# Two key masks on ScalarE, and weight sums and counts at other places, in a routed attention and experts kernel

## The chip, the cores and the metric

The kernel runs on one core of a Trainium2 chip. The metric is the device time of one execution in microseconds (us), as the median of several runs. One further execution was taken by the hardware profiler; its times of single instructions are the ones used here. TensorE (PE; PEld is its weight load) multiplies matrices, VectorE (DVE), ScalarE (ACT) and GpSimd (POOL) work elementwise, and SyncE (SP) issues most transfers. Each engine works through its own list of instructions in order and waits for others by semaphores.

## The reference

The reference is an attention whose queries and keys see each other only within one of 16 clusters, and behind it a layer of 8 experts in which each token goes to one of them:

```python
# q, k, v: (4, 8, 768, 64); centroids: (8, 16, 64)
q_assign = argmax(einsum('bhsd,hcd->bhsc', q_n, c_n)); k_assign likewise
scores = where(q_assign == k_assign, q @ k.T / 8, -1e9)
x = softmax(scores) @ v                      # -> x: (3072, 512)
expert = argmax(x @ w_gate)                  # 8 experts
y = relu(x[rows of e] @ w1[e]) @ w2[e]       # 512 -> 1024 -> 512
out = softmax(x @ w_gate)[expert] * y
```

## The kernel before

**Attention.** Two heads make a pair, and there are 16 pairs. A pair is worked in two halves of 384 queries (h) and six blocks of 128 keys (j). `score` (L438) gives one PSUM tile per (h, j): four float matmuls of keys and queries, then two bfloat16 matmuls of a key mask MK and a query mask MQ, which add nothing within a cluster and a large negative number outside it. ScalarE takes the exponential (L445), which frees the tile; there are three such tiles. `add_up` (L447) sums the exponentials on VectorE, and `attend` (L453) multiplies them by V after all twelve scores. The masks of the next pair are made meanwhile: `assign0` to `assign2` (L299 to L327) find each row's cluster on VectorE and leave it transposed as ohT, and `place` (L329) writes MK and MQ on ScalarE.

The first pair has no such cover. `start_first` (L345) works it in two halves of rows: `clusters(h)` (L388) does the assignment of one half and then `place_half` (L373) writes the masks of that half, spread over the engines. An index g names a strip: 0 and 1 are query strips, 2 and 3 key strips, and a is the head. Key masks of even g are written by VectorE, of odd g by GpSimd (L383); of the query masks of the first half, strip 0 is written by ScalarE and strip 1 by GpSimd (L380), those of the second half by GpSimd.

**Experts.** The tokens are handled in ten groups, s = 0 to 9, each of one expert and of a fixed size: `EARLY` = 288, 288 and `RANKED` = 256, 288, 288, 384, 416, 416, 448, 128 rows. Groups 0 and 1 use tokens of the first three batches only, so that they can start while the last batch's routing is still being computed inside group 0. All groups but the last compute the first layer (`layer1`, L948) by a form of Strassen's scheme: twice (j = 0, 1) seven products of quarter matrices on TensorE (L969). It needs sums of quarters of the weights, `w1_sums` (L809), A[2], A[1], A[0], A[3] in this order, and of the transposed rows, `turn_rows` (L776, xT) and `x_sums` (L791, xc). From group 1 on, each pair of row tiles of the second layer (`layer2`, L1052, products at L1070) does the same with `w2_sums` (L913, V[0] to V[3]; V[1] needs V[0], V[3] needs V[1]) and `h_sums` (L1026). Rows beyond that pair go through `tile_of` (L1081, matmuls at L1089): 32 or 64 rows within the pair's work, a whole tile of 128 behind it. All sums are made by VectorE through `strassen` (L788).

In both layers a product goes on adding to a PSUM bank that another engine has to read first. In `layer2` the products come in the order a, d, b, a, c, d, c. The addition `add(z1[:, H:], c, p7)` (L927 in the profile) reads bank c between its two products, and the second c product waits for it. `layer1` has the same place with `add(block(1, 1), ...)`.

**The order of other work.** It is written out by hand. After each product `hook()` runs a list of functions: h1 is the first layer's list of lists (14 places, 0 to 6 for j = 0, 7 to 13 for j = 1), h2 the second layer's. Place 1 of a pair in `layer2` lies behind the d product, 2 behind b, 3 behind a, 4 behind the first addition to z1, 5 behind the second, 6 behind the last c product. The functions of a place are issued in the order in which `at(list, place, function, ...)` (L1172) entered them. For the sums of the next group the tuple `when` (L1214 to L1218) gives six places, for A[2], A[1], A[0], A[3], V[2], V[0]. Groups with s >= 2 take the third tuple if the next group has 256 rows or more, so 2 to 7 do. `turn_rows` stands at place 3 of h2 and `x_sums` at 4 (for group 1 both at 1).

Within group 0, `choose` (L564) ends with the tile `last`, `count` (L588) multiplies it on TensorE (L592, L593), and `number` (L595) turns the counts into places, from which GpSimd writes the tokens' entries (L607). Beside them stand `weigh` (L755, xw) and the sums of group 1. Group 0's second layer has no pairs; its places come after every second of eight steps of a whole tile.

Of the kernel before, what the change touches and what calls it, by code (L numbers as in the profile page):

```python
# [12 lines left out]
AF = mybir.ActivationFunctionType  # L13
# [20 lines left out]
def kernel(  # L34
# [11 lines left out]
    nc = tc.nc  # L46
    B, H, S, D = q.shape
# [120 lines left out]
    with tc.manual_schedule(), ExitStack() as actx:  # L168
# [103 lines left out]
        QT, KT, SIM, OH = {}, {}, {}, {}  # L272
# [8 lines left out]
        ksc2 = consts.tile([P, 2], F32)  # L281
        kscn2 = consts.tile([P, 2], F32)
# [16 lines left out]
        def assign0(n, part=1):  # L299

            sim = asg.tile([P, HI, 2 * C], F32, name="sim")[:, 0 : HI // part]
            nc.vector.transpose(sim.rearrange("p i c -> p (i c)"), SIM.pop(n)[:, 0 : HS // part])
            SIM[n] = sim.rearrange("p i (a c) -> p (i a) c", c=C)
# [41 lines left out]
        def start_first():  # L345
            HQ = HS // 2
            cps = ps_m.tile([P, 512], F32, name="mps")
            ps = [ps_s.tile([P, 2, 512], F32, name="sps") for _ in range(2)]
            src = [d.pop(0) for d in (QIN, KIN)]
            dst = [qkt.tile([P, S], F32, name=name) for name in ("qT", "kT")]  # L350
            QT[0], KT[0] = dst

            def turned(w, h):
                for j in range(NQ // 2):
                    for a in range(2):
                        nc.tensor.matmul(  # L356
                            ps[w][D * a : D * (a + 1), h, P * j : P * (j + 1)], lhsT=src[w][:, a, NQ // 2 * h + j, :], rhs=ident,
                            start=True, stop=True,
                        )

            def copied(w, h):
                nc.scalar.copy(dst[w][:, HS * h : HS * (h + 1)], ps[w][:, h, 0:HS])

            def similar_half(h):
                sps = SIM[0] = ps_m.tile([P, 512], F32, name="mps")
                for g in range(4):
                    c0 = HS * h + HQ * (g % 2)
                    nc.tensor.matmul(
                        sps[Q4 * g : Q4 * (g + 1), 0:HQ], lhsT=cT[:, 0].rearrange("p a c -> p (a c)"),
                        rhs=dst[g // 2][:, c0 : c0 + HQ], start=True, stop=True,  # L370
                    )

            def place_half(h, w):  # L373
                for g in (2 * w, 2 * w + 1):
                    for a in range(2):
                        c0 = HS * h + HQ * (g % 2)
                        to = (MQ, MK)[w][0][D * a : D * a + Q4, c0 : c0 + HQ]
                        rows = slice(Q4 * g, Q4 * (g + 1))
                        if w == 0:
                            (nc.gpsimd.tensor_copy if h or g else nc.scalar.copy)(to, OH[0][rows])  # L380
                        else:

                            (nc.gpsimd if g % 2 else nc.vector).tensor_scalar(  # L383
                                to, OH[0][rows], scalar1=ksc2[rows, a : a + 1], scalar2=kscn2[rows, a : a + 1],
                                op0=ALU.mult, op1=ALU.add,
                            )

            def clusters(h):  # L388
                assign0(0, 2)
                assign1(0, 2)  # L390
                assign2(0, 2)
                for w in (h, 1 - h):
                    place_half(h, w)

            turned(0, 0)
            copied(0, 0)
            turned(1, 0)
            copied(1, 0)
            warm = consts.tile([P, 1], F32)
            nc.scalar.activation(warm, cnrm, AF.Exp, scale=0.0)  # L400
            nc.tensor.transpose(cps[:, 0:P], cn.rearrange("p a d -> p (a d)"), ident)
            cv = cps[:, 0:P].rearrange("p (h a c) -> p h a c", a=2, c=C)
            for a in range(2):
                nc.vector.tensor_copy(cT[D * a : D * (a + 1), :, a, :], cv[D * a : D * (a + 1), :, a, :])
            turned(0, 1)
            copied(0, 1)
            similar_half(0)
            turned(1, 1)
            copied(1, 1)
            clusters(0)  # L410
            score_half(0, 0, 0, True)
            similar_half(1)
            for j in (1, 2):
                score_half(0, 0, j, True)
            clusters(1)
            OH.pop(0)
            for a in range(2):
                nc.sync.dma_start(
                    out=cn_d.rearrange("(h a) d c -> a d h c", a=2)[a], in_=cT[D * a : D * (a + 1), :, a, :]
                )  # L420
# [474 lines left out]
    with tc.manual_schedule(), ExitStack() as ectx:  # L895
# [265 lines left out]
        def first_weights(s):  # L1161
            if s >= len(EARLY):
                expert(s)
            GR[s]["w1"] = fetch1(GR[s]["e"], (wa, wb)[s % 2])

        def second_weights(s):
            GR[s]["w2"] = fetch2(GR[s]["e"], (wa, wb)[s % 2])

        for s in range(NS):
            h1, h2 = {}, {}  # L1170

            def at(d, i, f, *a):  # L1172
                d.setdefault(i, []).append(lambda: f(*a))

            if s == 0:
                at(h1, 3, sum_up, n - 1)
                at(h1, 3, weights_of, n - 1)
                at(h1, 4, gate, B - 1)
                at(h1, 4, gate_exp, B - 1)
                at(h1, 5, gate_sum, B - 1)  # L1180
                at(h1, 5, choose, B - 1)
                at(h1, 8, count, B - 1)
                at(h1, 9, number, B - 1)
                at(h1, 11, rows, n - 1)
                at(h1, 11, store, n - 1)
                at(h1, 12, rank_all)
                at(h2, 0, rank_rest)
                at(h2, 3, places, 2)
                at(h2, 3, first_weights, 2)
                at(h2, 5, places, 3)  # L1190
                at(h2, 7, indices, 2)
                at(h2, 7, gather, 2)
            if s == 3:
                at(h1, 12, ask)
                at(h2, 4, answer)
            if s < last:
                if s == 0:
                    first_weights(1)
                elif s > 1:
                    take(s + 1)  # L1200
                if s == 1:
                    at(h1, 6, weigh, 2)
                    at(h1, 7, take, 2)
                    at(h1, 8, second_weights, 2)
                else:
                    second_weights(s + 1)
                if 0 < s <= last - 2:
                    at(h2, 0, first_weights, s + 2)

                if 0 < s <= last - 3:  # L1210
                    at(h2, 1, places, s + 3)

                if s == 0:
                    when = ((h2, 1), (h2, 2), (h2, 5), (h2, 6), (h2, 7), (h2, 7))  # L1214
                elif s == 1:
                    when = ((h1, 9), (h1, 12), (h2, 2), (h2, 3), (h2, 6), (h2, 6))
                else:
                    when = ((h1, 9), (h1, 10), (h2, 1), (h2, 2), (h2, 2), (h2, 5))  # L1218
                if GR[s + 1]["T"] >= 2 * P:
                    for (h, i), f, a in zip(when, (w1_sums,) * 4 + (w2_sums,) * 2, (2, 1, 0, 3, 2, 0)):  # L1220
                        at(h, i, f, s + 1, (a,), nc.vector)
                at(h2, 1 if s == 1 else 3, turn_rows, s + 1)
                if GR[s + 1]["T"] >= 2 * P:
                    at(h2, 1 if s == 1 else 4, x_sums, s + 1)
            if s == 0:
                at(h1, 2, gather, 1)
                at(h1, 8, weigh, 1, slice(0, 1))
                at(h1, 11, weigh, 1, slice(1, 2))
                at(h1, 12, weigh, 1, slice(2, 3))
                at(h1, 12, take, 1)  # L1230
            elif s + 2 <= last:
                at(h1, 5 if s == 2 else 4, indices, s + 2)
                at(h1, 5 if s == 2 else 4, gather, s + 2)
                at(h2, 6 if s == 1 else 4, weigh, s + 2)
            if pairs_of(s):
                at(h1, 4, w2_sums, s, (1,), nc.vector)

                at(h1, 5 if s == 1 else 6, w2_sums, s, (3,), nc.vector)
            if s == last - 1:

                at(h1, 4, nc.gpsimd.drain)
            (layer1 if GR[s]["T"] >= 2 * P else few_columns)(s, h1)
            h_sums(s)
            layer2(s, h2)
# [271 lines left out]
```

## Time and profile before

| | |
|---|---|
| median of 3 runs | 657.68 us (657.41 to 657.73) |
| the profiled execution | 657.44 us, its span 655.7 us |
| mean granted TensorE clock | 0.999 |
| attention, first pair to first expert product | 0 to 328.4 us |
| expert group 0 | 328.4 to 360.15 us |
| groups 1 to 9 | 360.15 us to the end |
| W1 or W2 sum on VectorE (L789, 128x1024) | 1.20 to 1.23 us |
| exponential on ScalarE (L445, 128x768) | 0.81 us |
| key mask, 32x192: VectorE / GpSimd (L383) | 346 / 504 ns (median) |
| key mask, 32x384: ScalarE (L340) | 700 ns |
| query mask, 32x192 / 32x384: ScalarE (L380, L337) | 350 / 510 ns |

A line of a timeline reads: start in us from the span's start, duration in us, engine, line, operation, output <- inputs, shapes, count (xN merges N in a row, and the duration runs from the first start to the last end), and in brackets the idle time of the engine in front of it and what ended it. Matmuls are pipelined, so neighbouring rows of PE overlap; the distance from start to start is the step. A float matmul counts as two.

### The profile page before, as it was taken

Reading aid. Unit: us, or ns where it says so; the run is one execution under the profiler, and the core shown is the slowest. Engines: PE = TensorE matmul, PEld = TensorE weight load, DVE = VectorE, ACT = ScalarE, POOL = GpSimd, SP = SyncE. Lnnn points to the kernel's source line nnn. Section 1 sums busy time; section 2 is a strip of 40 time slices with the busy share of each in tenths; the row PEclk is TensorE's granted clock in tenths of the full one; section 3 lists DMA queues with packets and bytes.
Section 4 is the critical chain, followed back from the end, with each engine's and each line's share of the span. In section 5 each row is a group of like instructions: output and inputs, shape, how many; then the busy total and the mean of one; then the engine's idle time right before and its main releaser. Section 6 shows DMA issues by size and latency. Waiting matters only on the chain.

```text
span 655.7 us, 11490 instructions
## 1 busy us (share of the span) xinstructions
PE 643.5 (98%) x4252; PEld 423.0 (65%) x4252; DVE 489.5 (75%) x845; ACT 338.3 (52%) x584; POOL 133.0 (20%) x166
## 2 busy tenths in 40 slices
PE   8999999999999999999999999999999999999995
PEld 4454544445444454444494989989897977869773
DVE  6988878998889988999977987888869365572300
ACT  5677877768778677867532433334241331413210
POOL 5500000022000300033013612324241422140010
PEclk9999999999999999999999999999999999999999
DMA  7753445443455433329476498667694836614010
GB/s 150 162 104 73 79 92 98 74 80 62 79 98 98 74 74 72 74 33 334 110 274 195 152 335 283 232 254 234 241 309 157 281 131 184 229 66 168 8 49 19
DMA packets 189760, 95.38 MB, mean 145 GB/s; under 512 B 152895, under 2 KB 171839, under 8 KB 188416
## 3 DMA queue, kind: packets, MB, share of 16 engines
q1 hardware_dynamic: 184624, 81.56, 45.4%
q0 software_dynamic: 4928, 12.97, 6.0%
q8 instruction: 35, 0.57, 0.4%
q14 instruction: 29, 0.24, 0.1%
q10 hardware_dynamic: 144, 0.03, 0.0%
HBM read 74.10 MB, written 20.70 MB: 145 GB/s over the span
## 4 chain that ended last, share of the span: by engine, by line
PE 94%; DVE 4%; issue 0%; ACT 0%; POOL 0%; POOLq 0%; DVEq 0%; ACTq 0%
PE sps L433 24%; PE mps L457 19%; PE bank L969 12%; PE bank L1089 10%; PE sbank L969 9%; PE bank L1070 7%; PE sbank L1070 6%; PE mps L480 3%; PE mps L291 2%; PE bank L938 1%; DVE xT L780 1%; DVE a L789 1%; DVE v L789 1%; PE sps L356 0%; PE sps L226 0%
## 5 line engine op out<-in xcount | busy, mean ns | idle before, releaser
L445 ACT ACTIVATE A<-sps 128x768 f32<-128x768 f32 x192 | 151.7, 814 | 29.1 <-PE sps L433 28.5
L433 PE MATMUL sps<-qT,kT 64*128 64x384 f32 x768 | 158.9, 492 | 0.0
L451 DVE TENSOR_TENSOR acc<-acc,A 128x768 f32<-128x768 f32 x128 | 121.3, 948 | 10.6 <-ACT A L445 2.4
L457 PE MATMUL mps<-A,v_in 128*64 128x384 f32 x768 | 127.4, 488 | 0.0
L433 PEld LDWEIGHTS sps<-qT,kT 64*128 64x128 f32 x768 | 66.8, 187 | 52.2 <-issue 46.0
L457 PEld LDWEIGHTS mps<-A,v_in 128*64 128x64 f32 x768 | 53.8, 137 | 70.6 <-issue 64.2
L1044 POOL DMA_INDIRECT out_dram<-z,si x30 | 47.1, 1571 | 195.3 <-DVE z L927 165.7
L607 POOL DMA_INDIRECT tokens_of<-tg,pos_i x24 | 28.2, 1176 | 268.5 <-DVE pos_i L605 262.4
L433 PE MATMUL sps<-mq,mk 64*128 64x384 bf16 x384 | 64.6, 323 | 1.6 <-DVE mk L383 1.0
L1089 PE MATMUL bank<-w,h 128*128 128x512 f32 (+2 forms) x224 | 64.4, 596 | 0.0
L340 ACT ACTIVATE mk<-ohT,kscn,ksc 32x384 bf16<-32x384 bf16 x60 | 42.0, 700 | 40.2 <-DVE ohT L327 36.3
L738 POOL DMA_INDIRECT xg<-x_rows,gi x30 | 40.3, 1343 | 45.8 <-DVE si L729 16.5
L969 PE MATMUL sbank<-xc,a 128*128 128x144 f32 (+4 forms) x288 | 47.9, 309 | 0.2 <-ACT sbank L1002 0.2
L969 PE MATMUL bank<-xT,w 128*128 128x144 f32 (+4 forms) x288 | 47.6, 308 | 0.0
L1089 PEld LDWEIGHTS bank<-w,h 128*128 128x128 f32 (+2 forms) x224 | 24.6, 151 | 32.5 <-issue 32.3
L969 PEld LDWEIGHTS bank<-xT,w 128*128 128x128 f32 x288 | 43.8, 190 | 2.3 <-issue 1.9
L451 DVE TENSOR_TENSOR acc<-A 128x768 f32<-128x768 f32 x32 | 30.6, 957 | 18.3 <-ACT A L445 18.2
L969 PEld LDWEIGHTS sbank<-xc,a 128*128 128x128 f32 x288 | 43.3, 190 | 0.7 <-ACT sbank L1002 0.4
L927 DVE TENSOR_TENSOR h<-sbank,p 128x288 f32<-128x288 f32 (+4 forms) x18 | 9.2, 513 | 45.3 <-PE sbank L969 43.9
L987 ACT ACTIVATE h<-h 128x288 f32<-128x288 f32 (+4 forms) x36 | 17.6, 488 | 40.2 <-DVE h L927 38.1
L433 PEld LDWEIGHTS <-mk 64*128 64x128 bf16 x384 | 19.9, 94 | 27.5 <-DVE mk L383 2.6
L755 DVE TENSOR_TENSOR xw<-xg,sf 128x256 f32<-128x256 f32 (+2 forms) x60 | 32.6, 603 | 0.2
(216 smaller groups left out, 898.7 us busy)
## 6 DMA issues: line engine op xcount, KB each, us to landing
w<-in_moe_w_dram SPq DMA_DIRECT2D x20, 2048.0 KB
v_in<-in_v_dram SPq DMA_DIRECT2D x32, 192.0 KB
x_rows<-x SPq DMA_DIRECT2D x64, 96.0 KB
turn_rows<-xw SPq DMA_DIRECT2D x23, 256.0 KB
q_in<-in_q_dram SPq DMA_DIRECT2D x60, 96.0 KB
k_in<-in_k_dram SPq DMA_DIRECT2D x60, 96.0 KB
xs<-turn_rows SPq DMA_DIRECT2D x16, 144.0 KB
xs<-turn_rows SPq DMA_DIRECT2D x8, 208.0 KB
```

The costliest lines, as they stand in the source:

```text
L340: nc.scalar.activation(dst, src, AF.Identity, bias=less, scale=big)
L433: nc.tensor.matmul(SP[n, h, j][:, a, 0:HS], lhsT=kt[rows, j * P : (j + 1) * P], rhs=qt[rows, h * HS : (h + 1) * HS], start=first, stop=not ...
L445: nc.scalar.activation(A[n, h, j], ps[:, :, 0:HS], AF.Exp, scale=D**-0.5)
L451: nc.vector.tensor_tensor(ACC[n, h], first, A[n, h, j], op=ALU.add)
L457: nc.tensor.matmul(O[n, h][D * a : D * (a + 1), 0:HS], lhsT=VIN[n][:, a, j, :], rhs=A[n, h, j][:, a, :], start=(j == 0), stop=(j == NQ - 1),)
L607: ins = nc.gpsimd.indirect_dma_start(out=t_d[:, :], out_offset=bass.IndirectOffsetOnAxis(ap=pos_i[:, i : i + 1], axis=0), in_=tg[:, b, i, ...
L738: nc.gpsimd.indirect_dma_start(out=xg[0:m], out_offset=None, in_=x_d[0:rows_in, :], in_offset=bass.IndirectOffsetOnAxis(ap=g["gi"][0:m, j ...
L755: nc.vector.tensor_tensor(xw[0:m, :, :, d2 * a : d2 * (a + 1)], xg[0:m].rearrange("p (r a d b) -> p a r b d", r=HP, a=2, b=DB)[:, a], g["s ...
L969: nc.tensor.matmul(ps[:, f * T2 : (f + 1) * T2], lhsT=w[:, k, (2 * j + f) * P : (2 * j + f + 1) * P], rhs=x[:, k, :], start=first and f + ...
L1044: ins = nc.gpsimd.indirect_dma_start(out=out[:, :], out_offset=bass.IndirectOffsetOnAxis(ap=GR[s]["si"][0:rows, j : j + 1], axis=0), in_=z ...
L1070: nc.tensor.matmul(ps[:, 0:H], lhsT=x[:, k, :], rhs=y[:, k, :], start=first and k == 0, stop=k == 3, skip_group_check=not first,)
L1089: nc.tensor.matmul(ps[i * m : (i + 1) * m, :], lhsT=h[:, f, j * P : j * P + m], rhs=w[:, f, :], start=(k == 0), stop=(k == FB // n - 1),)
```

## The change

Three places. In `place_half` the two key masks of strip 2 of the first half (h = 0) are written by ScalarE, as an Identity activation with the same scale and bias. In group 0, `count` and `number` stand one place later. And two of the `when` tuples change: for group 0 A[1] moves from place 2 to 1, A[0] from 5 to 2, A[3] from 6 to 2 and V[2] from 7 to 6; for groups 2 to 7 V[2] moves from 2 to 5 and V[0] from 5 to 6.

```diff
                         if w == 0:
                             (nc.gpsimd.tensor_copy if h or g else nc.scalar.copy)(to, OH[0][rows])
+                        elif h + g == 2:
+
+                            nc.scalar.activation(
+                                to, OH[0][rows], AF.Identity, bias=kscn2[rows, a : a + 1], scale=ksc2[rows, a : a + 1]
+                            )
                         else:
-
                             (nc.gpsimd if g % 2 else nc.vector).tensor_scalar(
...
-                at(h1, 8, count, B - 1)
-                at(h1, 9, number, B - 1)
+                at(h1, 9, count, B - 1)
+                at(h1, 10, number, B - 1)
...
                 if s == 0:
-                    when = ((h2, 1), (h2, 2), (h2, 5), (h2, 6), (h2, 7), (h2, 7))
+                    when = ((h2, 1), (h2, 1), (h2, 2), (h2, 2), (h2, 6), (h2, 7))
                 elif s == 1:
                     when = ((h1, 9), (h1, 12), (h2, 2), (h2, 3), (h2, 6), (h2, 6))
                 else:
-                    when = ((h1, 9), (h1, 10), (h2, 1), (h2, 2), (h2, 2), (h2, 5))
+                    when = ((h1, 9), (h1, 10), (h2, 1), (h2, 2), (h2, 5), (h2, 6))
```

## The prediction

> **What bounds the kernel now.** I read the page's busy shares first, then the chain of work that ended last, then the waits of TensorE, and then the timeline around each wait.
>
> ```profile
> PE 643.5 (98%) x4252; PEld 423.0 (65%) x4252; DVE 489.5 (75%) x845; ACT 338.3 (52%) x584; POOL 133.0 (20%) x166
> ...
> PE 94%; DVE 4%; issue 0%; ACT 0%; POOL 0%; POOLq 0%; DVEq 0%; ACTq 0%
> ```
>
> TensorE is busy for 643.5 of 655.7 us and carries 94% of the chain. The granted clock is 0.999. No edit here removes a matmul, so only the roughly 12 us in which TensorE stands still can be won. The waits of TensorE (us in total, times, longest) say where:
>
> ```profile
> PE sbank L1070 <- DVE z L927: 1.2, 4, 0.4
> PE sps L433 <- DVE mk L383: 1.0, 1, 1.0
> PE mps L592 <- DVE last L586: 0.6, 1, 0.6
> PE sbank L969 <- DVE h L927: 0.5, 1, 0.5
> ```
>
> All four end on VectorE, and each edit lies beside one of them. A wait is worth more than its number, because the overlap of neighbouring matmul groups is lost too. So I measure each from starts to starts in the timeline, against the same step where it runs unhindered.
>
> **Start: two key masks go to ScalarE.** The timeline of before:
>
> ```profile
> 10.81 0.72 ACT L380 COPY mq<-ohT 32x192 bf16<-32x192 bf16 x2 [1.50 <-DVE ohT L327]
> 10.88 0.82 DVE L383 TENSOR_SCALAR mk<-ohT,ksc,kscn 32x192 bf16<-32x192 bf16 x2
> ...
> 12.13 0.81 ACT L445 ACTIVATE A<-sps 128x768 f32<-128x768 f32 x1 [0.60 <-PE sps L433]
> ...
> 14.67 0.68 DVE L383 TENSOR_SCALAR mk<-ohT,ksc,kscn 32x192 bf16<-32x192 bf16 x2
> ...
> 15.04 0.70 PE L433 MATMUL sps<-mq,mk 64*128 64x384 bf16 x2 [1.00 <-DVE mk L383]
> ```
>
> VectorE loses the two masks of 10.88, and its next work, the second half's assignment (11.73 on), waits for nothing else: it moves up by 11.73 - 10.88 = 0.85 us. The second half's masks are then ready for TensorE at 14.2 instead of 15.04.
>
> ScalarE gains two masks behind its two query copies, in front of the first exponential. This shape has no row there. The copies give the slope: 510 ns at 384 columns, 350 at 192, so 160 for 192 columns. The mask of 384 columns (L340) takes 700, so 192 take an estimated 540 ns. Bounds: 350 (the copy, no multiply) and 700. The masks run from 11.55 to 12.65. In before the second one ended at 11.70 and the exponential began 0.43 later, so it now begins at about 13.08 and ends at 13.89. Its end frees the PSUM tile for the fourth score matmul (13.07 before, 0.13 after the first exponential's end): 14.02. The mask matmul follows 0.65 to 0.75 later: 14.7 instead of 15.04. ScalarE agrees: two more exponentials (1.51) end at 15.42, against the 15.77 at which the fourth began. Gain 0.35 us; with 350 ns per mask 0.7, with 700 none. GpSimd's mask work (11.74 to 12.84) is not moved and still ends in front of the third score's need.
>
> Here a rule speaks against the change: the Trainium skill, page "ScalarE: Activation LUTs", section "Rules for kernel authors", sends multiplies and adds to VectorE, up to about three times as fast per element in bf16. The row has a median of 346 ns on VectorE, so by three times a mask would cost 1040 on ScalarE, the exponential would start 1.0 us later than I have it, and the start would lose 0.65. I take the slope of the rows, which gives a factor of 1.6.
>
> One more wait follows. In the second pair the step from the first score group to the sums takes 31.00 to 33.96, in the third pair 51.08 to 53.70: 0.34 more, because ScalarE's query masks come late behind "DVE ohT" (its 28.14 row waits for that). VectorE has no idle gap between 11.73 and 28.02, so that transpose comes 0.85 us earlier while TensorE comes 0.35 earlier. The 0.34 goes. Start in all: 0.7 us (0 to 1.1). The loads don't hold it: the first 14 us moved 2.4 MB, all that these transposes read.
>
> **First expert group: count and number one product later.**
>
> ```profile
> 339.10 0.17 DVE L586 CAST last<-pr 128x8 bf16<-128x8 f32 x1
> 339.19 1.13 DVE L755 TENSOR_TENSOR xw<-xg,sf 128x256 f32<-128x256 f32 x2
> 339.33 0.17 PE L592 MATMUL mps<-last,lt_b 128*128 128x8 bf16 x1 [0.59 <-DVE last L586]
> ```
>
> The product that starts at 337.59 ends its step at 338.57 (0.98 each), then TensorE waits for "last". The next product could run: it needs nothing of VectorE. Moved in front, it ends its step at 339.55, after "last" (339.27). From 337.59 to the product at 340.44 are 2.85 us; two products and about 0.1 for the count matmuls are 2.06. Gain 0.79. The step "number" reads the count on VectorE at 340.22, behind the xw pair there; its place in VectorE's order doesn't change (the built order shows it), and the count is ready at about 339.85. So its six indirect writes, and the SyncE loads behind them, are not later. The cover is 0.28 us; without it some of the wait returns.
>
> **First group, second layer: weight sums earlier.** Two W1 sums move in front of the transpose xT, where VectorE waits 3.67 us for the DMA of xs (355.81): 2.4 us of work, hidden. Behind the x sums then stand only two W2 sums.
>
> ```profile
> 363.93 2.35 DVE L789 TENSOR_TENSOR v<-w 128x1024 f32<-128x1024 f32 x2
> ...
> 366.20 0.45 DVE L927 TENSOR_TENSOR h<-sbank,p 128x288 f32<-128x288 f32 x1
> ...
> 366.71 1.25 PE L969 MATMUL sbank<-xT,a 128*128 128x144 f32 x8 [0.52 <-DVE h L927]
> ```
>
> Without the 2.4 us the addition of 366.20 comes when its product ends, at 365.2, and TensorE doesn't wait. 365.05 to 367.79 is 2.74, unhindered 1.96: gain 0.78. Both w2 and w1 of this group have landed by 342 (DMA idle then), so the earlier sums don't wait for them. The index steps for group 2's gather now have one sum (1.2) in front of them rather than two W1 sums, so GpSimd's gather and what SyncE issues behind it come no later.
>
> **Groups 2 to 7: one W2 sum leaves the place in front of xT.**
>
> ```profile
> 466.27 1.21 DVE L789 TENSOR_TENSOR v<-w 128x1024 f32<-128x1024 f32 x1
> 467.19 1.89 PE L1070 MATMUL bank<-v,h 128*128 128x256 f32 x8
> 467.40 1.76 DVE L780 STREAM_TRANSPOSE xT<-xs 128x1536 f32<-128x1536 f32 x1
> 469.10 0.37 DVE L927 TENSOR_TENSOR z<-sbank,p 128x256 f32<-128x256 f32 x1
> 469.52 1.99 PE L1070 MATMUL sbank<-w,hs 128*128 128x256 f32 x8 [0.44 <-DVE z L927]
> ```
>
> The last product writes the bank that "z" reads, so it waits for VectorE's queue. The step from the product before it to the product after it, less two free steps of 1.73: group 2, 3.85 - 3.46 = 0.39; group 4, 4.17 - 3.46 = 0.71; group 6, 0.48; group 7, 0.61; groups 3 and 5 nothing (0 to 0.1). Taking a sum (1.13 from start to start) out is more than any of these: in group 4 "z" starts at 467.97 and must end by 468.92. In group 2 the sum also waits 1.95 us for its weights, which no longer stands in front. Gain 2.19. What is late next: both W2 sums (2.3 us) now stand behind "z<-bank,u", and the next group's first addition behind them. VectorE's total in front of that addition is the same as before, but TensorE arrives earlier. Group 4 has 0.76 us of idle there and TensorE comes 0.71 earlier; group 2 keeps about 0.3; group 3 has 0.32 and TensorE comes no earlier; groups 5 to 7 have a whole output tile (6.87) between. No cost, but it is tight. Of the queues, SyncE alone changes its order: one load of a word of xe falls behind three writes of turned rows, which are issued earlier; nothing there is near TensorE.
>
> **Sum.** 0.69 + 0.79 + 0.78 + 2.19 = 4.45 us. The profiled execution took 657.44 (span 655.7), so 653.0; the median of the runs is 657.68, so 653.2. What a measurement can tell from no change is 0.2%, 1.3 us.
>
> **Rivals.**
> *The start gives nothing.* ScalarE's masks cost 700 ns or more and the first exponential eats what VectorE wins. For it: the first exponential then stands behind four operations instead of two. Against: the slope. Time: 657.68 - 3.76 = 653.9; by the rule's 1040 ns 654.2 (1.0 of the 4.45 lost).
> *The experts' stalls come back.* The tight places of groups 2 to 4 each take back what the group won, or the count waits again: about half of 3.76 is lost, 655.1. For it: the covers of 0.05 to 0.3 us. Against: behind the addition there are some 0.5 us more until TensorE needs it.
> *Slower.* The pair of W2 sums becomes a block in front of the next group's addition in groups 2, 3 and 4, which have no output tile in between. To lose it must cost 2.4 us per sum rather than 1.2 (contention with GpSimd's writes that start there): 3 x (2.4 - 0.5) = 5.7 lost against 4.45 won, 658.9. It decides once the block ends some 2 us later than I have it. Against: the 1.20 to 1.23 of every such row.
> *It does not do what it says*: the built order shows each move, so I give this no time of its own.
>
> **How the numbers follow.** All parts as computed 0.56; start without gain 0.16; stalls half back 0.16; within 0.2% 0.06; slower 0.06. Faster by over 0.2% is 0.88. The range goes from 652.2 (start at its best, and the 0.2 wait of L1002 gone too) to 655.8.
>
> **What would show it.** TensorE's waits on L383, L592, "h" L927, and all but one of those on "z" L927 (group 1 stays) gone; the mask matmul of 15.04 at about 14.7; the first exponential near 13.1; the mask row on ScalarE near 540 ns. Wrong if "sbank L969 <- DVE h" grows in groups 3 to 5, or the fourth exponential is not earlier than 15.77.

## The result and the profile after

The changed kernel takes 651.76 us (median of 6 runs, 651.37 to 652.41) against 657.69 us (657.08 to 658.26) of before in the same runs: a ratio of 0.9912 (95% interval 0.99 to 0.9924), so 5.9 us less (5.0 to 6.6). The forecast was 653.2 with a range from 652.2 to 655.8. The gain was there, and larger: 5.9 us where 4.45 were foretold, and the time lies just below the range.

The page's busy line of after, and the waits of TensorE (us in total, times, longest):

```profile
PE 641.4 (99%) x4252; PEld 422.9 (65%) x4252; DVE 488.6 (75%) x843; ACT 339.7 (52%) x586; POOL 139.1 (21%) x166
```

```profile
PE sps L226 <- DVE mq L219: 1.4, 1, 1.4
PE sps L437 <- ACT mk L383: 0.8, 2, 0.6
PE sps L437 <- ACT A L449: 0.3, 1, 0.3
PE sbank L1074 <- DVE z L931: 0.2, 1, 0.2
```

(Lines behind the edit stand 4 later than in before.) TensorE is busy for 641.4 us in a span of 650.6. All four waits that the prediction read out are gone: on VectorE's mask (1.0), on "last" (0.6), on "h" (0.5), and of those on "z" only group 1's 0.2 is left. Gone too are 0.5 on GpSimd's masks and 0.2 on L1002. New are 0.8 and 0.3 on ScalarE, in the first pair. The timeline of after there:

```profile
10.94 0.38 DVE L327 STREAM_TRANSPOSE ohT<-oh 128x192 bf16<-128x192 bf16 x1
...
12.09 1.10 ACT L383 ACTIVATE mk<-ohT,kscn,ksc 32x192 bf16<-32x192 bf16 x2
...
13.62 2.92 ACT L449 ACTIVATE A<-sps 128x768 f32<-128x768 f32 x4 [0.43 <-PE sps L437]
...
14.48 0.92 PE L437 MATMUL sps<-qT,kT 64*128 64x384 f32 x4 [0.25 <-ACT A L449]
15.23 0.33 PE L437 MATMUL sps<-mq,mk 64*128 64x384 bf16 x2
15.39 0.81 PE L437 MATMUL sps<-qT,kT 64*128 64x384 f32 x4
```

This execution began 0.54 us late: ohT is at 10.94, in before at 10.40 (the first transposes on TensorE took longer; in the other profiles ohT lies between 9.69 and 10.99). In the frame of before the first exponential starts at 13.62 - 0.54 = 13.08 and the mask matmul at 14.69. And group 4's second layer, where before had a W2 sum at 466.27 in front of xT:

```profile
462.77 1.76 DVE L784 STREAM_TRANSPOSE xT<-xs 128x1536 f32<-128x1536 f32 x1
464.05 1.89 PE L1074 MATMUL bank<-v,h 128*128 128x256 f32 x8
464.46 0.37 DVE L931 TENSOR_TENSOR z<-sbank,p 128x256 f32<-128x256 f32 x1
...
465.77 1.89 PE L1074 MATMUL sbank<-w,hs 128*128 128x256 f32 x8
```

"z" is done at 464.83, 0.94 us ahead of the product that needs it, and that product starts one free step (1.72) behind the one before.

The starts of TensorE's products, after against before, give this sum (us):

| step | foretold | measured in the traces |
|---|---|---|
| first pair, from ohT to the first sums | 0.35 | 0.61 |
| second pair | 0.34 | 0.34 |
| count and number | 0.79 | 0.76 |
| sums in group 0 | 0.78 | 0.78 |
| groups 2, 4, 6, 7 | 0.39, 0.71, 0.48, 0.61 | 0.40, 0.70, 0.49, 0.62 |
| group 3, first layer | none | 0.48 |
| pair 14 to pair 15 | none | 0.31 |
| sum | 4.45 | 5.49 |

Less the late beginning (0.54) that is 4.95; TensorE's last block of products starts at 637.12 instead of 642.08, 4.96 earlier.

### The profile page after: what moved, and what is told of

Same layout as the page of the kernel before. It is cut to its first block, busy times and chain, and to the rows that moved or that the text cites. A ratio compares the mean times of both kernels' runs of the same rounds, so it can differ in the third digit from the quotient of the medians.

```text
span 650.6 us, 11481 instructions
## 1 busy us (share of the span) xinstructions
PE 641.4 (99%) x4252; PEld 422.9 (65%) x4252; DVE 488.6 (75%) x843; ACT 339.7 (52%) x586; POOL 139.1 (21%) x166
## 4 chain that ended last, share of the span: by engine, by line
PE 98%; DVE 1%; ACT 0%; issue 0%; POOL 0%; POOLq 0%; DVEq 0%
PE sps L437 25%; PE mps L461 19%; PE bank L973 13%; PE bank L1093 10%; PE sbank L973 10%; PE bank L1074 8%; PE sbank L1074 6%; PE mps L484 3%; PE mps L291 2%; PE bank L942 1%; PE sps L356 1%; PE sps L226 0%; DVE a L793 0%; ACT mk L383 0%; ACT A L449 0%; PE sbank L907 0%
## 5 line engine op out<-in xcount | busy, mean ns | idle before, releaser
L1048 POOL DMA_INDIRECT out_dram<-z,si x30 | 52.0, 1732 | 188.1 <-DVE z L931 161.2
L742 POOL DMA_INDIRECT xg<-x_rows,gi x30 | 40.2, 1342 | 42.5 <-DVE si L733 14.3
```

The costliest lines, as they stand in the source:

```text
L742: nc.gpsimd.indirect_dma_start(out=xg[0:m], out_offset=None, in_=x_d[0:rows_in, :], in_offset=bass.IndirectOffsetOnAxis(ap=g["gi"][0:m, j ...
L1048: ins = nc.gpsimd.indirect_dma_start(out=out[:, :], out_offset=bass.IndirectOffsetOnAxis(ap=GR[s]["si"][0:rows, j : j + 1], axis=0), in_=z ...
```

## The experiments

Fifteen runs on four chips. In the expectations letters name theories; each expectation says what its letter means. Times are medians, gains are worked out from the ratio to before on the same chip and its interval, and need not equal the difference of the medians. The question of the first four: which part holds the excess?

**e1_masks**: before with the diff of `place_half` alone.

> Only the two key masks on ScalarE. Theory A (the four parts add up; what the prediction missed lies in small waits it did not count): the start is worth 0.95 us, the 0.69 foreseen and 0.26 that was missed because the second mask of the second half made TensorE wait once more (15.04 to 15.40), so 656.7. Theory B (the rest of the gain is an accident of the two profiled executions and the runs around them): 0.69, so 657.0. Theory C (the missed 1.5 us sit in the start, which the profile of the changed kernel hides by a later start): 655.5 or less. In the profile: the step from the second pair's first scores to its sums 2.62 instead of 2.96 under all of them.

656.47 us against 658.28: 2.1 us faster (1.4 to 2.8). More than the 0.95 that the first two pairs of the traces of before and after show, or the 1.26 with pair 15.

**e2_count**:

```diff
-                at(h1, 8, count, B - 1)
-                at(h1, 9, number, B - 1)
+                at(h1, 9, count, B - 1)
+                at(h1, 10, number, B - 1)
```

> Only count and number one place later. A and B: 0.79 us less, 656.9; the wait of L592 gone, nothing later in the trace changed. If the missed gain sat here (an earlier start of something that depends on the counts): 656 or less.

657.32: 0.9 us faster (0.3 to 1.6), in the trace 0.76.

**e3_group0**:

```diff
-                    when = ((h2, 1), (h2, 2), (h2, 5), (h2, 6), (h2, 7), (h2, 7))
+                    when = ((h2, 1), (h2, 1), (h2, 2), (h2, 2), (h2, 6), (h2, 7))
```

> Only the sums' places in group 0. A and B: 0.78 us less, 656.9; the wait of the product of 366.71 gone, the other waits as before.

657.44: 0.7 us faster (1.5 to none). As expected, though the interval does not exclude nothing.

**e4_groups27**:

```diff
-                    when = ((h1, 9), (h1, 10), (h2, 1), (h2, 2), (h2, 2), (h2, 5))
+                    when = ((h1, 9), (h1, 10), (h2, 1), (h2, 2), (h2, 5), (h2, 6))
```

> Only the places of the two W2 sums in groups 2 to 7. A and B: 2.19 us less, 655.5, in groups 2, 4, 6 and 7 with 0.39, 0.71, 0.48 and 0.61. If the 0.48 of group 3's first layer (the wait of L1002 at 425.38 in before) belongs to this edit, 655.0 and that wait is gone here and still there in the other three.

655.58: 3.2 us faster (2.1 to 4.3). In its trace the groups give 0.40, 0.48 (group 3), 0.70, 0.49 and 0.62, so 2.7. Group 3's step is thus part of this edit.

The profile of e4, which has VectorE's masks, showed something that the profile of before had not: from 15.3 to 18.7 us TensorE had half its clock. From this came theory D: TensorE's standstill there lets the clock fall in some executions.

**c_nomasks**: the changed kernel without the diff of `place_half`.

> The changed kernel with the two key masks back on VectorE: everything but the start's edit. Theory A (each part is worth what the traces' starts show, 0.95 us for the masks: 0.61 in the first pair, 0.34 in the second, and 0.3 more near pair 15): 0.95 to 1.25 us slower than the changed kernel, so about 5.0 us faster than before. Theory D (without the mask edit TensorE stands still around 11 to 15 us, and in some executions the granted clock then falls to 0.50 for 3.3 us, which costs 1.6 us when it happens): 1.3 to 2.5 us slower than the changed kernel in the median, with a wider spread, and mean clocks down to 0.994 in some of its runs where the changed kernel never falls under 0.997. In the profile: the wait of TensorE for the mask of VectorE at 15 us is back (1.0 us), the first step of the second pair is 2.96 again, and the step from pair 14 to 15 is 20.27 again rather than 19.95.

**p_after**: the changed kernel again, on the chip of c_nomasks.

> The changed kernel again, on the chip of the other three. Theory A: 5.2 us faster than before (start 0.95, pair 15 0.3, count 0.76, group 0 0.78, groups 2 to 7 2.2 without the wait of group 3, and up to 0.5 for that one). Theory D: up to 6.9 us, the sum of the four single edits on their chip, where before shows its wider spread. In the profile no clock under 1.0 in the first 26 us, and the end of the query copies of GpSimd at 2.3 us again rather than 1.5.

c_nomasks takes 653.61 us (652.93 to 654.02), p_after 651.49 (651.01 to 652.35), before 657.6. So the masks are worth 2.1 us here too, and the two ranges do not touch; this is what theory D expected (1.3 to 2.5) and more than A did. p_after is 6.2 us faster than before (5.0 to 7.4), which does not tell the two apart. In the profile of c_nomasks VectorE's mask holds TensorE for 1.0 us again and the step from pair 14 to 15 is 20.27, as expected; but the step of the second pair stays at 2.62, where 2.96 was expected (see p_before). The stretches of c_nomasks (busy of each engine, then the granted clock in the third column from the end, DMA share, GB/s):

```profile
14.00:15.00 1.00, 0.27 (x1) 0.09 (x1) 0.93 (x3) 0.47 (x1) 0.55 (x1) 1.00 0.35 45
15.00:16.00 1.00, 0.97 (x6) 0.69 (x7) 0.97 (x3) 0.54 (x1) 0.84 (x2) 0.68 0.16 12
16.00:17.00 1.00, 1.00 (x7) 0.69 (x4) 1.00 (x3) 0.27 (x1) 0.90 (x3) 0.50 0.19 25
17.00:18.00 1.00, 1.00 (x5) 0.47 (x4) 0.90 (x2) 0.81 (x1) 0.95 (x1) 0.50 0.00 0
18.00:19.00 1.00, 1.00 (x8) 0.86 (x6) 0.90 (x2) 0.40 (x1) 0.86 (x4) 0.61 0.00 0
```

TensorE stands still for 0.73 us of the stretch from 14 to 15, the last part of a gap of 1.00, and 0.6 us behind it the clock falls to 0.50, from 15.36 to 18.77. That is 3.41 us, not the 3.3 that the expectations have, and it is 3.41 in all five profiles that show a fall at the start. In p_after it is busy for 0.75 there, and the clock stays:

```profile
14.00:15.00 1.00, 0.75 (x5) 0.40 (x6) 0.90 (x4) 1.00 (x3) 0.80 (x2) 1.00 0.33 40
15.00:16.00 1.00, 1.00 (x10) 0.50 (x8) 1.00 (x2) 1.00 (x3) 0.90 (x3) 1.00 0.12 17
```

From ohT to the first sums are 14.40 us in c_nomasks, 13.2 in seven profiles with VectorE's masks and no fall of the clock, 12.71 in the one profile of before that the prediction had, and 12.0 to 12.1 with ScalarE's masks written once.

**f_fill**: before, with idle matmuls in the gap.

```diff
+            if n + h == 0 and j == 3:
+                for _ in range(14):
+                    nc.tensor.matmul(SP[-1][:, 0, HS:512], lhsT=MK[1][:, 0:P], rhs=MQ[1][:, 0:P], start=True, stop=True)
             score_half(n, h, j, False)
...
```

(`SP[-1]` is the tile of the score before.)

> Before, with 14 small bfloat16 matmuls (128 columns, zeros, into columns that nothing reads) put on TensorE in front of the first score that waits for VectorE's mask of the second half, where it stands still from 14.0 to 15.0 us. They take an estimated 0.8 us of that gap and release nothing. Theory A (only the waits count): same as before, within 0.3 us. Theory D (the standstill lets the clock fall in some executions): the clock never falls at 15 us in any run, no mean clock under 0.997, and the median is 0.5 to 1.5 us faster than before.

656.39: 1.2 us faster (0.7 to 1.7), but not as meant. The matmuls waited 0.79 us for the exponential that reads that tile, the clock fell in the profile at 14.3 all the same, and they put the masked score 1.3 us later. In its profile three waits of the experts (0.8, 0.4 and 0.5 us in groups 0, 2 and 3) were absent, which nothing in the edit explains; such waits come and go from one execution to the next, as is shown below. As a test of D it failed. Still, of its 22 runs the profiled one alone has a mean clock of 0.996 or less.

**g_fill2**: 8 matmuls, into a tile that ScalarE doesn't read.

```diff
...
+            if n + h == 0 and j == 3:
+                for _ in range(8):
+                    nc.tensor.matmul(SIM[-1][:, HS:512], lhsT=MK[1][:, 0:P], rhs=MQ[1][:, 0:P], start=True, stop=True)
```

(`SIM[-1]` is the tile of the first pair's second similarities.)

> As f_fill, but with 8 matmuls, and into columns of a PSUM tile that ScalarE does not read, so that they need not wait for an exponential (in f_fill they did, from 13.61 to 14.40, and then ran at half clock and put the masked score 1.3 us later). Theory D (TensorE's standstill ahead of 15 us lets the clock fall to a half for 3.3 us in most executions of before): the masked score is at the time of before (1.0 us behind the end of the fourth first-half score, within 0.2), no clock under 1.0 in the first 26 us, and the median is 0.8 to 1.6 us faster than before. Theory A (waits alone): the same as before within 0.3 us. If the clock falls all the same, a standstill of 1 us at 14 us is not what brings it about.

657.43: 0.7 us faster (0.2 to 1.3), no fall of the clock in its profile, and the masked score waits 0.4 us instead of 1.0. None of its 13 runs has a mean clock of 0.996 or less; of 133 runs of before on the four chips 47 have, and every profile that shows the fall does. The clock is kept, but the gain is under the 0.8 to 1.6 that D expected: between A and D.

**s_double**: the changed kernel, with each ScalarE mask written twice.

```diff
...
+                            for _ in range(2):
+                                nc.scalar.activation(
+                                    to, OH[0][rows], AF.Identity, bias=kscn2[rows, a : a + 1], scale=ksc2[rows, a : a + 1]
+                                )
```

> The changed kernel, with each of the two ScalarE masks written twice (the same values), so 1.1 us more on ScalarE in front of the first exponential. By the prediction's chain (first exponential, PSUM tile, fourth score, mask matmul) the first exponential comes 1.1 us later, at about 14.2 by the clock of before, the fourth score too, and the start loses 1.1 us against the changed kernel. Rival: TensorE is held by VectorE's and GpSimd's masks of the second half, not by the tile, and loses under 0.4. Theory D adds: the longer standstill can bring the half clock back, so 2 us and more in some runs.

653.99 us (653.28 to 654.31), 2.5 us above p_after, or 1.5 by the ratios to before (another chip, so roughly). Its timeline and stretches:

```profile
10.83 2.25 ACT L383 ACTIVATE mk<-ohT,kscn,ksc 32x192 bf16<-32x192 bf16 x4
...
13.51 2.22 ACT L449 ACTIVATE A<-sps 128x768 f32<-128x768 f32 x3 [0.42 <-PE sps L437]
...
14.37 1.65 PE L437 MATMUL sps<-qT,kT 64*128 64x384 f32 x4 [0.57 <-ACT A L449]
```

```profile
14.00:15.00 1.00, 0.63 (x2) 0.50 (x4) 0.97 (x2) 1.00 (x3) 0.84 (x3) 0.67 0.29 36
15.00:16.00 1.00, 1.00 (x6) 0.34 (x4) 1.00 (x2) 0.73 (x2) 0.89 (x3) 0.50 0.24 26
```

From ohT (9.69) to the exponential are 3.82 us, in after 2.68: the 1.1 us of two more masks, in full, and from the exponential on they reach TensorE. The prediction's chain holds. And the longer standstill (2.5 us of gaps instead of 1.0) brings the half clock back, in a kernel that never showed it: ohT to the first sums is 14.79, 2.7 more than in after, 1.1 for the masks, so 1.6 for the clock.

**e5_two**: before, two clears moved off VectorE's program, and one load moved.

```diff
-        for t in (MQ[0], MK[0]):
-            nc.vector.memset(t, 0.0)
+        nc.vector.memset(MQ[0], 0.0)
+        nc.gpsimd.memset(MK[0], 0.0)
...
-        nc.vector.memset(cT, 0.0)
+        nc.gpsimd.memset(cT, 0.0)
...
+                elif s == 2:
+                    at(h1, 11, second_weights, 3)
                 else:
                     second_weights(s + 1)
```

> Before, with two moves that have nothing to do with the change's wording: two clears of VectorE's first instructions (of a mask tile and of cT) go to GpSimd, which shortens VectorE's program by two instructions as the mask edit does; and the 2 MB load of the second weights for group 3 is issued later, at step 11 of group 2's first layer... that is of the group before, in front of it nothing waits. If the late kT of pair 15 comes from a gap at one place in VectorE's instructions (theory P): its step from 280.48 to 300.75 is 19.95 instead of 20.27, as with the mask edit. If it comes from the masks' own timing: 20.27. If TensorE's late products near 425 in the following layer come from that load (theory W): the wait on the ScalarE copy of L1002 (0.2, in all 0.48) is gone; if not, it stays. Both: 0.8 us faster than before; neither: the same within 0.3.

657.35: 1.0 us faster (0.5 to 1.5). The step from pair 14 to 15 is 19.96, not 20.27. In before VectorE has a gap there that nothing releases, in e5_two, in e1_masks and in after it has none:

```profile
276.96 0.17 DVE L605 TENSOR_SCALAR pos_i<-pos 128x6 int32<-128x6 f32 x1
277.35 0.96 DVE L451 TENSOR_TENSOR acc<-acc,A 128x768 f32<-128x768 f32 x1 [0.21 <-issue]
```

```profile
276.90 0.17 DVE L605 TENSOR_SCALAR pos_i<-pos 128x6 int32<-128x6 f32 x1
276.98 0.95 DVE L451 TENSOR_TENSOR acc<-acc,A 128x768 f32<-128x768 f32 x1
```

(Before first, then e5_two.) The gap costs VectorE 0.3 us, the next pair's keys are turned late, and TensorE waits. It goes with two instructions fewer in VectorE's program, whichever they are, the two masks or two clears: theory P. The trace shows a transfer on an instruction queue in the same microsecond; that it is the cause is only argued. Theory W was not tested: the load that I moved is group 3's own, and the one near 421 us is group 4's. A gap of 0.4 stays in group 3.

**p_before**: before, unchanged, one more profiled execution.

> Before again, one look. Theory D: the half clock near 15 to 18 us is seen in this profile as in two of the four kernels without the mask edit that were profiled so far besides before itself; if it is not, its time should be nearer to 656 than to 659. The wait of TensorE near 425 and the late kT of pair 15 recur at the same places if they are the program's, and do not if they are chance.

660.32 us, 2.9 more than the first profile (0.9 of it can be the chip, by the medians of before), and without a fall of the clock, against what D expected of so slow an execution. The late keys of pair 15 and the wait of group 3 recur. Its waits:

```profile
PE sbank L1070 <- DVE z L927: 2.4, 5, 1.2
...
PE sbank L969 <- DVE h L927: 0.9, 1, 0.9
PE sbank L969 <- ACT sbank L1002: 0.8, 1, 0.8
```

The same program waits 1.2 on "z" in group 2, where the first profile shows no wait above its threshold (a step 0.39 too long), 0.9 instead of 0.5 on "h", and 0.8 instead of 0.2 on L1002. Its first two pairs, before (the same program) in front:

```profile
15.94 1.49 POOL L380 COPY mq<-ohT 32x192 bf16<-32x192 bf16 x4
...
31.00 0.92 PE L433 MATMUL sps<-qT,kT 64*128 64x384 f32 x4
...
33.96 0.86 PE L480 MATMUL mps<-acc,ones_s 128*32 128x192 f32 x16
```

```profile
16.53 2.32 POOL L380 COPY mq<-ohT 32x192 bf16<-32x192 bf16 x4
...
18.90 0.32 PE L433 MATMUL sps<-mq,mk 64*128 64x384 bf16 x1 [0.23 <-POOL mq L380]
...
32.06 0.92 PE L433 MATMUL sps<-qT,kT 64*128 64x384 f32 x4
...
34.68 0.86 PE L480 MATMUL mps<-acc,ones_s 128*32 128x192 f32 x16
```

GpSimd's query copies take 2.32 us instead of 1.49 and hold a score, so the first pair ends 0.5 later, and the second pair's step is 2.62 instead of 2.96. It is 2.62 in all sixteen profiles other than the first one of before. So the 0.34 that the prediction counted there belonged to that one execution.

With this the other profiles can be read. For "h" in group 0, VectorE's idle time in front of xT (for the DMA of xs) against TensorE's wait, in all kernels without that edit:

| VectorE waits for xs, us | 2.7 | 2.9, 2.9 | 3.1 | 3.5 | 3.6 | 3.7 | 3.8 | 4.1 | 4.2 | 4.3 |
|---|---|---|---|---|---|---|---|---|---|---|
| TensorE waits on "h", us | 0 | 0 | 0 | 0.4 | 0.5 | 0.5 | 0.7 | 0.9 | 1.0 | 1.2 |

The wait is what the landing of xs exceeds 3.1 us by, to 0.1 us. In the six kernels with the edit, VectorE has two sums (2.3 us) to do in that time, still waits (1.4 in after), and TensorE never waits. Group 2's wait goes the same way with VectorE's idle time in front of the V[2] sum: a step 0.1 too long or none for 1.0 to 1.7 us of idle, 0.4 for 1.95, 0.8 for 2.4 and 1.5 for 3.0. With the edit nothing waits for that sum.

**x_fifth** and **x_sixth**: before, with one of the two entries.

```diff
-                    when = ((h1, 9), (h1, 10), (h2, 1), (h2, 2), (h2, 2), (h2, 5))
+                    when = ((h1, 9), (h1, 10), (h2, 1), (h2, 2), (h2, 5), (h2, 5))
```

```diff
-                    when = ((h1, 9), (h1, 10), (h2, 1), (h2, 2), (h2, 2), (h2, 5))
+                    when = ((h1, 9), (h1, 10), (h2, 1), (h2, 2), (h2, 2), (h2, 6))
```

> Before, and of the edit for groups 2 to 7 only the fifth entry: the first W2 sum goes from product 2 to product 5 of layer 2 (behind z), the second stays at 5 behind it. The prediction puts the whole 2.19 us on the sum that stands in front of xT and z, and that is this one. Theory F: the waits on z in groups 2, 4, 6 and 7 are gone, 0.4, 0.7, 0.5 and 0.6, so all of 2.2 us, as in the run with both; the wait of group 3's first layer (0.5) tells by itself whether it belongs to this sum. Rival: the second sum at 5 now stands in front of the next group's first addition, half of the gain is lost, and the sixth entry is what brings the rest.

> Before, and only the sixth entry: the second W2 sum one product later, 6 in place of 5. Theory F: no wait on z changes, so the same as before within 0.3 us. If the wait of group 3's first layer near 425 is gone here and stays with the fifth entry alone, it belongs to what is queued behind the second sum; if it stays here and is gone there, to the first.

x_fifth: 655.45 against 659.01, 3.6 us faster (2.6 to 4.4), with 0.40, 0.48, 0.70, 0.49 and 0.62 in the groups' traces, as with both entries. x_sixth: 658.5, the same (1.1 faster to 0.2 slower), with the waits of groups 3, 4, 6 and 7 in place. The term belongs to the sum in front of xT, and the second move does nothing.

**x_gather**: before, group 5's gathers later.

```diff
-                at(h1, 5 if s == 2 else 4, indices, s + 2)
-                at(h1, 5 if s == 2 else 4, gather, s + 2)
+                at(h1, 9 if s == 3 else 5 if s == 2 else 4, indices, s + 2)
+                at(h1, 9 if s == 3 else 5 if s == 2 else 4, gather, s + 2)
```

> Before, with the three row gathers of group 5 by GpSimd, and the two index steps in front of them, five products later in group 3's first layer (9 in place of 4), where they no longer lie at 421 to 425 us. Theory G (TensorE's late products there come from these gathers, which run beside them in before but start a microsecond later with the W2 edit): the wait of 0.2 to 0.8 us on the copy of L1002 is gone, 0.5 us faster than before. Rival (they have nothing to do with it): it stays, or shows as a gap of TensorE that nothing releases, and the time is the same within 0.3 us.

657.25 against 659.01: 2.0 us faster (1.4 to 2.6). In its trace group 3's first layer is 0.48 shorter than in before; group 2's step is 0.3 shorter, by its own changing wait, and the other steps of groups 1 to 7 stay. Before, then x_gather:

```profile
421.18 0.98 POOL L738 DMA_INDIRECT xg<-x_rows,gi  x1 [0.30 <-issue]
...
425.38 1.25 PE L969 MATMUL sbank<-xc,a 128*128 128x144 f32 x8 [0.21 <-ACT sbank L1002]
```

```profile
425.26 1.84 POOL L738 DMA_INDIRECT xg<-x_rows,gi  x1 [2.95 <-DVE si L729]
425.45 1.14 PE L969 MATMUL sbank<-xc,a 128*128 128x144 f32 x8
```

Group 4's 2 MB load still starts beside it (421.52), so the load alone is not the cause. With the V[2] edit the gathers come later too: GpSimd's first write in front of them takes 2.89 us instead of 1.75, and the first gather starts 2.2 us behind the start of the product sbank<-xT,a (417.44 in after) in place of 1.1 (420.11 in before). One kernel (f_fill) has early gathers and no late product. So the gathers are part of the cause, and how they hold up TensorE stays open. The 0.48 of the first profile is small for this stop: over the nine profiles with V[2] and the gathers at their old places group 3's first layer is longer than unhindered by 0.86 us on average (none to 1.19). Why the runs show 2.0 us stays open.

**b1_group1**: the changed kernel, with one more tuple.

```diff
-                    when = ((h1, 9), (h1, 12), (h2, 2), (h2, 3), (h2, 6), (h2, 6))
+                    when = ((h1, 9), (h1, 12), (h2, 4), (h2, 5), (h2, 6), (h2, 6))
```

> The changed kernel, and in group 1 the third and fourth W1 sum one or two products later in layer 2 (4 and 5 in place of 2 and 3), so that nothing stands in front of the addition z that TensorE still waits for there (0.2, the last of the waits on z). Expected: 0.4 us faster than the changed kernel, because that step is 0.42 longer than an unhindered one. Rival: the two sums then stand in front of the first addition of group 2, and TensorE waits there instead, so no gain or up to 0.5 us slower.

652.09 (651.7 to 652.37) against 651.49 of p_after on that chip: no gain. The wait on "z" is gone, and a new one stands in group 2's first layer:

```profile
PE sbank L972 <- DVE h L930: 0.4, 1, 0.4
```

This is the rival that the prediction named for groups 2 to 4, where it did not come true. No version here beats the changed kernel.

## Why the prediction was right in its mechanism and short in its sum

Two terms of the sum failed, both too small. The start, put at 0.69 us, is worth about 1.8; and group 3, put at nothing, had a stop in its first layer that the edit takes away, 0.48 us in the first profile and 0.86 on average. The waits named and the ways by which they go were right, and the other terms came to 3.4 us against the 3.8 foretold.

*What was right.* Between the traces of before and after every step that it named came out within 0.03 us, but for the first pair: second pair, count, group 0, groups 2, 4, 6 and 7. For the second pair, group 0 and group 2 this is in part luck, since these waits are others in other executions. The mask on ScalarE was put at 540 ns (row of after: 1.10 for two, 550), the first exponential at 13.08 (13.08), the mask matmul at 14.7 (14.69). Against the row of VectorE's masks, 346, the factor is 1.6, not the three of the rule that spoke against the change. That rule counts per element; by the two copies of the table (350 and 510 ns) an estimated 190 of 350 ns are there at any width, so it should not have been put on the whole row.

*Start, first pair: the term of 0.35 measured 0.61.* It ended at the first masked score of the second half. But before had a second stop 0.36 us later, for the second mask (its weight load on TensorE waits 0.27 for mk). In after the two scores are 0.16 apart, because both masks were written well ahead. That is 0.20 of the missing 0.26; I had read only the row with the longest wait.

*Start, in most executions of before: more than any trace term.* "The granted clock is 0.999" was read from one execution. Of twelve profiles of kernels with VectorE's masks four show the half clock for 3.41 us behind the gaps of the first pair, which costs 1.2 us there; the other seven beside before run that stretch in 13.2, not 12.71 (GpSimd's query copies, 2.32 us instead of 1.49, then hold a score for 0.2). Of the four profiles with ScalarE's masks written once none shows the fall, and of the 30 runs of these kernels none has a mean clock of 0.996 or less. So the edit is worth 13.2 - 12.05 + 0.31 (pair 15) = 1.5 us without the fall and 2.7 with it, and measured 2.1 in both ways of asking. The Trainium skill, page "TensorE: Matmul & The Clock Gate", section "What's actually happening", says that the clock is set from how busy the array has been lately, in a window of 3413 ns that runs freely; the falls of 3.41 us agree. That the same gaps fall into one window in some executions and into two in others would explain why only some show a fall, but no run here shows it. Its section "Why this matters for your kernels" asks for no gaps over about 3 us; here gaps of 0.2, 0.3 and 1.0 us within some 3 us were enough, so by the rule the start had nothing to lose, and by the stretches it had 1.2. A doubt remains: of the seventeen profiles the five with this fall have a mean clock of 0.996 or less, and the twelve without it have more; yet the runs of before with such a mean are only 0.4 us slower than the rest on their chip. What one fall costs is thus shown in traces, not in medians.

*Pair 15, no term, measured 0.31.* The prediction said of VectorE's two instructions only what they cost. That their absence shifts everything behind them in its program, and takes away a gap 265 us later, can be seen from no row of before; e5_two shows that two other instructions do the same.

*Group 3: no term, measured 0.48.* "Groups 3 and 5 nothing" held for the step that it was said of, the second layer's. The 0.2 wait on L1002 in group 3's first layer was kept only for the low end of the range, as chance. It goes with the V[2] sum (x_fifth), and it goes with GpSimd's gathers issued later (x_gather). (That low end is itself off: a start of 1.1 and the 0.2 added to the sum give 652.6, not 652.2.)

*The sum of one execution.* Each of the waits was sized from one profile. The edits do not take away a fixed number; in groups 0 and 2 they take away the reach of a late DMA. An estimate from the means of all profiles that have a step unchanged, less those that have it changed (9 to 11 against 4 to 7), is this (us):

| step | foretold | mean of the profiles |
|---|---|---|
| start: first pair, second pair, pair 15 | 0.69 | 1.77 |
| count and number | 0.79 | 0.76 |
| sums in group 0 | 0.78 | 0.67 (none to 1.42) |
| group 2 | 0.39 | 0.29 (none to 1.48) |
| group 3, first layer | none | 0.86 (none to 1.19) |
| groups 4, 6 and 7 | 1.80 | 1.72 |
| sum | 4.45 | 6.07 |

The runs gave 5.9 (5.0 to 6.6) and 6.2 (5.0 to 7.4). So the waits for late DMAs, sized from one execution, were not what fell short; they came out a little high. These means are of single executions on several chips, gathered after the result.

*The rivals.* Start gives nothing: no. Stalls come back: not in groups 2 to 4, yes in b1_group1. Slower: the pairs of W2 sums took 1.20 to 1.23 each.

## What to carry to other kernels

Size a wait that ends on a DMA from several executions, or at least say how late the transfer may come before the wait begins; an edit that puts other work in that gap is worth the mean of the waits, not the one seen (here none to 1.4 us, and 0.67 on average, for one and the same wait). When TensorE's short gaps lie close together, look at the granted clock by the microsecond in more than one profile: here shortening them took away 3.4 us of half clock, 1.2 us of time, that one profile did not show. And when taking a first stop away, look for the second stop right behind it.

## What the runs showed of the hardware

- Gaps of TensorE that add up to 1.3 to 1.5 us within some 3 us were followed in four of eleven profiles by a granted clock of 0.50. Gaps of 0.9 (g_fill2) and 1.0 us (ScalarE's masks) were not, in five profiles; and of the 43 runs of these kernels none has a mean clock of 0.996 or less, where 47 of 133 runs of before have. Gaps of 2.5 us (s_double) were followed by it.
- Each of the five falls at the start lasted 3.41 us.
- Two instructions fewer in VectorE's program removed a gap of 0.2 us that stood about 265 us later, and 0.3 us of TensorE's step behind it.
- An Identity activation with scale and bias of 32x192 in bf16 took 550 ns on ScalarE, a plain copy 350, VectorE's tensor_scalar 346.
- GpSimd's first indirect write of group 3 took 2.89 us in all profiles with the V[2] sum moved behind z, and 1.75 in all others.
